# Six tiles of q and k in block 0: turned by VectorE in 32x32 blocks from finer loads, not by TensorE transposes with ScalarE copies

## The chip, the cores and the metric

One core of one Trainium2 chip. The metric is device time in microseconds (us). Engines are called TensorE (PE; its weight loads PEld), VectorE (DVE), ScalarE (ACT), GpSimd (POOL) and SyncE (SP, which here only issues DMAs).

## The reference, cut to what matters

```python
def sm_attn(qq, kk, vv):
    s = scale * np.matmul(qq, kk.transpose(0, 1, 3, 2))
    s = s - np.max(s, axis=-1, keepdims=True)
    a = np.exp(s)
    a = a / (np.sum(a, axis=-1, keepdims=True) + 1e-09)
    return np.matmul(a, vv)
p_packed = sm_attn(p, k, v)              # p: 8 x 8 heads x 32 x 64
out = sm_attn(q, p_packed, p_packed)     # q, k, v: 8 x 8 heads x 576 x 64
...
h = x @ w_in;  g = h / (1 + exp(-h));             x = g @ w_out      # first MLP
h = x @ w_in2; g = h * clip(h + 3, 0, 6) / 6;     y = g @ w_out2     # second MLP
```

x has 4608 rows of 512 numbers (8 batches x 576 positions, 8 heads x 64), and both MLPs widen it to 2048. All is float32.

## The kernel before, in words

The first MLP runs in nine blocks of 512 rows: block j takes the first 512 positions of batch j, the ninth the 64 left over from each batch. Within a block the 2048 wide columns go by in 16 steps f. hidden(f) makes 128 of them (lines 992 to 994, three products each, since every operand is kept as a high and a low part), ScalarE takes Silu (line 1001) and the high part gh (line 1008), VectorE the low part gl (line 1009), and two steps later projects(f) multiplies back into four accumulators (lines 1016 to 1018). Block 0 also makes the weights into high and low parts as it goes: for each f, ScalarE scales the raw words (lines 180 and 186), VectorE shifts and signs them (lines 195 and 199), GpSimd adds them (line 208), ScalarE rounds the sum to the high part (line 219) and VectorE subtracts (line 224). SyncE then stores the parts to memory for later blocks (line 215, tiles win, wo and wr). Each link waits for the one before it.

The attention of later batches is threaded through the blocks. A group n is four heads of a batch, so batch b has groups 2b and 2b+1. Groups 0 and 1 are done ahead of block 0; in block 0 comes the attention of groups 2 and 3, one after the other. A group has two tiles of q and two of k, each 128x512 for two heads. The steps of a group n in order: k is transposed and multiplied with p (scores), exponentials, the transposed weights a1 (tile T, made by line 431 through the copy of line 108), the products with v (lines 482 and 485), the packed keys, then q is transposed and multiplied with these, a second softmax, and the products that become x.

The class Plan places these steps between the MLP's products. A step has a place (a share of the block's products that must have gone by), needs (steps that must be so many products back), a tile limit and a number of PSUM banks that the planner's ring must have free. Four banks of tag h are shared by the hidden products and by all attention steps; a hidden bank comes free when gl of its step has been taken. What a step issues goes into its engines' in-order queues at that spot.

step_tr turns one tile of two heads (line 451). For groups up to 3 it takes four TensorE transposes into a PSUM bank (line 449) and a ScalarE copy to SBUF (line 108). For groups from 4 on it is one VectorE instruction that transposes each 32x32 block (line 456), which is the full transpose only because load_nat has put the 32x32 blocks where they belong: four DMAs of 32 partitions and 128-byte pieces (line 382) where the other form has two DMAs of 128 partitions and 256-byte pieces (line 386). The finer DMAs don't go out where load_nat is called: they stand in the list due, of which each tick of the planner issues one on SyncE's queue, and use() issues all that is left as long as the block is 0 or 1. SyncE also issues the weight stores and the loads of v. ScalarE issues the loads of raw weights in block 0 from its own queue (line 155).

Of the kernel before, what the change touches and what calls it, by code (L numbers as in the profile page):

```python
# [18 lines left out]
def tile_pack_attention_two_mlps(ctx: ExitStack, tc, q, k, v, p, w_in1, w_out1, w_in2, w_out2, out):  # L19
# [76 lines left out]
    def bank():  # L96

        pool, tag = (ps_h, "h")
        if early[0]:
            pool, tag = banks[0]  # L100
            banks.append(banks.pop(0))
        return pool.tile([P, T], F32, tag=tag, name="abank")
# [4 lines left out]
    def copy(out, in_):  # L107
        (nc.vector.tensor_copy if other[0] else nc.scalar.copy)(out=out, in_=in_)
# [10 lines left out]
    def half_kb(n, tag, bufs=1, what=""):  # L119

        if n == 1 or (n == 0 and what == "q"):
            pool, tag, n = spare.pop()
            if pool is xp:
                return pool.tile([P, T], F32, tag=tag, name="spare")
            if tag not in shared:
                shared[tag] = pool.tile([P, 2, T], F32, tag=f"wr{tag}", name="spare")
            return shared[tag][:, n]
        return at.tile([P, T], F32, tag=tag, name=tag, bufs=bufs)
# [222 lines left out]
    def ask(key=None):  # L351
        while due if key is None else any(k == key for k, _ in due):
            due.pop(0)[1]()
            if key is None:
                return
# [11 lines left out]
    def load_nat(n, what, j):  # L367
        src = {"k": k, "q": q, "v": v}[what]
        b, h0 = n // QPB, (n % QPB) * HQ + 2 * j
        m = half_kb(n, "nat", 2 * AHEAD, what)  # L370
        rows = src[b, h0:h0 + 2, 0:T, :]
        if what == "v":
            m = m.rearrange("p (h i d) -> p h i d", h=2, i=NI)
            load_queue[0].dma_start(out=m.rearrange("p h i d -> p h (i d)"), in_=rows.rearrange("h (p i) d -> p h (i d)", i=NI))
        elif n >= 4:

            g = m.rearrange("p (i b d) -> p i b d", i=NI, b=NI)
            for h in range(2):
                for e in range(2):
                    o = (2 * h + e) * NP  # L380
                    src = rows[h].rearrange("(b r i) d -> r i b d", b=NI, i=NI)[:, :, :, e * NP:(e + 1) * NP]
                    due.append(((what, n, j), lambda to=g[o:o + NP], src=src: nc.sync.dma_start(out=to, in_=src)))
        else:
            m = m.rearrange("p (i h d) -> p i h d", h=2, i=NI)
            for h in range(2):
                load_queue[0].dma_start(out=m[:, :, h, :], in_=rows[h].rearrange("(p i) d -> p i d", i=NI))
            m = m.rearrange("p i h d -> p i (h d)")
        nat[what, n, j] = m
# [58 lines left out]
    def turn_rows(ps, m):  # L447
        for i in range(NI):
            nc.tensor.transpose(ps[:, i * P:(i + 1) * P], m[:, i, :], ident)

    def step_tr(n, what, j):
        m = nat.pop((what, n, j))
        if n >= 4:
            ask((what, n, j))
            t = half_kb(n, "T", 5)
            nc.vector.transpose(out=t, in_=m)
            st[what, n, j] = t
            return
        ps = bank()
        turn_rows(ps, m)  # L460
        t = half_kb(n, "T", 5)
        copy(out=t, in_=ps)
        st[what, n, j] = t
# [117 lines left out]
    def step_u(n):  # L581
        ps = bank()
        nc.vector.transpose(out=ps, in_=d2s[n][:, 0:T])
        ah = at.tile([P, T], F32R, tag="a2h", name="a2h", bufs=3)
        al = at.tile([P, T], F32R, tag="a2l", name="a2l", bufs=3)
        copy(out=ah, in_=ps)
        nc.vector.tensor_sub(out=al, in0=ps, in1=f32(ah))
        st["a2", n] = ah, al

    def step_ut(n):  # L590
        assert st.pop("tails", None) is None
        st["tails"] = n
        for j in range(2):
            rows = slice(j * 64, (j + 1) * 64)
            nc.vector.transpose(out=tails[rows, j * TAIL:(j + 1) * TAIL], in_=d2s[n][rows, T:S])
# [128 lines left out]
    for j in range(2, B - 1):  # L724
        c, d = QPB * (j + 2), QPB * (j + 1)
# [14 lines left out]
    def load_next():  # L740

        while loaded[0] < len(uses) and (loaded[0] < AHEAD or uses[loaded[0] - AHEAD] in used):
            what, n = uses[loaded[0]]
            if what == "v" and any(w == "v" and (w, m) not in used for w, m in uses[:loaded[0]]):
                return
            loaded[0] += 1
            if what == "v" or what == "q" and n == QPB:
                load_tail(n, what)
            for j in range(2):
                load_nat(n, what, j)  # L750

    def use(what, n):
        used.add((what, n))
        load_next()
        while due and plan.block < 2:
            ask()
# [87 lines left out]
    def window(c, d, b, a, j, x):  # L844
# [6 lines left out]
        def add(n, what, cost, fn, *need, tile=None, bank=5, also=(), count=1):  # L851
            if n is not None:
                steps.append(((what, n), cost, fn, need, tile, bank, [k for k in also if k[1] is not None], count))
# [30 lines left out]
        add(c, "spread", 0, lambda: spread_p(c), ("kpq", b), bank=0)  # L884

        def turn():
            add(d, "q0", 0, lambda: step_tr(d, "q", 0), (("t", b if j == 1 else None), 0), bank=5 if j == 0 and (d or 9) < 4 else 0, tile=("z", d))
            add(d, "q1", 0, lambda: [step_tr(d, "q", 1), use("q", d)], ("q0", d), bank=5 if j == 0 and (d or 9) < 4 else 0, tile=("z", d))
            add(a, "u", 0, lambda: [step_u(a), step_ut(a)], before[1], (("t", b), 22 if j else 0), bank=15)
            add(c, "k0", 0, lambda: step_tr(c, "k", 0), (("q1", d), 0), (("t", b if j == 1 and d is not None else None), 20), bank=5 if j == 0 and (c or 9) < 4 else 0, tile=("s", c))  # L890
            add(c, "k1", 0, lambda: [step_tr(c, "k", 1), use("k", c)], ("k0", c), bank=5 if j == 0 and (c or 9) < 4 else 0, tile=("s", c))

        if j == 0:
            if b is not None:
# [2 lines left out]
            else:  # L897
                add(either, "kpq", 2, kpq, ("spread", c), bank=7)
            add(b, "pp", 4, lambda: step_pp(b), ("t", b), ("tt", b))
            turn()  # L900
            add(c, "s", 6, lambda: step_zs(c, None, None, None), ("k1", c), ("kpq", c), ("tt", b), bank=9, count=2, also=[("st", c)])
            add(b, "pt", 1, lambda: [alone(b, step_pt, step_ptc), use("v", b)], ("pp", b))
# [3 lines left out]
        else:  # L906
# [12 lines left out]
            if keys:  # L919
                n_banks = (b is not None) + (p0 is not None) + 1  # L920
                add(keys[0][1], keys[0][0], 2 * n_banks, transposes, before[0] if b is not None else ("spread", c), ("spread", c), ("pp", p0), tile=b is not None and ("pp", b),
                    bank=8, count=n_banks, also=keys[1:])
                add(x, "flush", 0, flush, ("xt", x), bank=0)
            b0 = b if j > 1 else None
            if j == 1:
                add(b, "pp", 4, lambda: step_pp(b), ("t", b), ("tt", b))
                p1 = b
            turn()

            def scores():  # L930
# [5 lines left out]
            if keys:  # L936
# [3 lines left out]
                    bank=9, also=keys[1:], count=n_banks)  # L940
# [765 lines left out]
    unit = [key for key in feed.keys]  # L1706

    load_nat(0, "k", 0)
    beside(load_p, 0)
    beside(load_nat, 0, "k", 1)  # L1710
    load_tail(0, "k")
    beside(load_nat, 1, "k", 0)
# [163 lines left out]
    for j in range(NBLK):  # L1876
        ws = WINDOWS[j] if j < len(WINDOWS) else []
        order = []
        n = QPB * (j + 1) - 1
# [118 lines left out]
```

## Time and profile before

| | |
|---|---|
| median of 3 runs | 1508.78 us (1508.05 to 1509.45) |
| the profiled execution: its own time, its span | 1509.61 us, 1507.8 us |
| busy in the span: PE, DVE, ACT, POOL | 98%, 69%, 52%, 13% |
| mean granted TensorE clock | 0.995 of full |

The span runs from the first to the last instruction; 1.8 us of the profiled execution's time lie around it. A matmul's row in the trace lasts longer than the distance to the next one, since matmuls are pipelined: how fast they go is read from their starts. Block 0 takes the stretch from about 36 to 160 us.

### The profile page before, as it was taken

The page shows a single profiled execution, that of the slowest core. Times are in us where ns is not written, and L with a number is a line of the kernel's source. Part 1 is how long each engine was busy: PE and PEld are TensorE (multiplying, and loading weights), DVE is VectorE, ACT ScalarE, POOL GpSimd, SP SyncE. Part 2 cuts the span into 40 slices and gives each one's busy share as a digit, 9 for nine tenths or more (in the row PEclk, how much of TensorE's full clock was granted, in tenths as well). Part 3 has the DMA queues.
Part 4 walks back from the last instruction along what each step waited for, and adds up shares of the span by engine and source line. Part 5 has one row for each costly group of instructions (what it writes and reads, how often), then busy time and mean ns, then how long its engine had stood idle before and what let it go on. Part 6 is the DMA issues. An engine that isn't in the chain of part 4 may idle for free.

```text
span 1507.8 us, 21726 instructions
## 1 busy us (share of the span) xinstructions
PE 1483.1 (98%) x7550; PEld 1230.3 (82%) x7550; DVE 1036.0 (69%) x1695; ACT 779.4 (52%) x1241; POOL 192.5 (13%) x177
## 2 busy tenths in 40 slices
PE   7999999999999999999999999999999999999998
PEld 4777777777777778788878888888888888999998
DVE  6767466756575656653463779786978687778767
ACT  6876657655566456655452344334433443444443
POOL 2433011111211211123240000000000000000000
PEclk9999999999999999999999999999999999999999
DMA  9999789997698769868895576678667866997987
GB/s 246 306 306 276 247 214 253 274 253 198 177 245 263 199 165 306 231 178 239 243 291 178 193 225 216 195 216 252 219 193 223 242 215 210 286 313 255 271 273 226
DMA packets 434509, 358.52 MB, mean 238 GB/s; under 512 B 191200, under 2 KB 325856, under 8 KB 434400
## 3 DMA queue, kind: packets, MB, share of 16 engines
q1 hardware_dynamic: 422832, 343.59, 77.6%
q10 hardware_dynamic: 11568, 13.54, 2.9%
q8 instruction: 61, 1.00, 0.3%
q14 instruction: 48, 0.39, 0.1%
HBM read 295.17 MB, written 61.87 MB: 237 GB/s over the span
## 4 chain that ended last, share of the span: by engine, by line
PE 84%; ACT 6%; DMA 4%; DVE 3%; SPq 2%; issue 1%; POOL 1%; ACTq 0%; POOLq 0%; DVEq 0%
PE b L1270 8%; PE b L1268 8%; PE b L1269 8%; PE b L1363 8%; PE b L1366 7%; PE b L1365 7%; PE acc L1016 7%; PE acc L1017 7%; PE acc L1018 7%; PE hps L992 4%; PE hps L993 4%; PE hps L994 4%; DMA wo<-w1o 1%; DMA praw<-in_moe_w_out_dram 1%; PE abank L524 1%
## 5 line engine op out<-in xcount | busy, mean ns | idle before, releaser
L1009 DVE TENSOR_TENSOR gl<-hps,gh 128x512 fp32r<-128x512 f32 x144 | 98.9, 687 | 190.6 <-ACT gh L1008 187.8
L1366 PE MATMUL b<-ro,ws 128*128 128x512 f32 (+2 forms) x564 | 206.4, 366 | 0.0
L1365 PE MATMUL b<-ro,ws 128*128 128x512 f32 (+2 forms) x564 | 206.3, 366 | 0.0
L1268 PE MATMUL b<-xc,ws 128*128 128x512 f32 (+1 forms) x560 | 205.7, 367 | 0.0
L1270 PE MATMUL b<-xc,ws 128*128 128x512 f32 (+1 forms) x560 | 205.7, 367 | 0.0
L1269 PE MATMUL b<-xc,ws 128*128 128x512 f32 (+1 forms) x560 | 205.7, 367 | 0.0
L1311 DVE TENSOR_TENSOR ro<-g,ro 128x1024 fp32r<-128x1024 f32 (+1 forms) x140 | 161.5, 1158 | 41.5 <-ACT ro L1306 41.2
L1306 ACT CAST ro<-g 128x1024 fp32r<-128x1024 f32 (+1 forms) x140 | 132.0, 967 | 93.4 <-DVE g L1299 34.5
L1001 ACT ACTIVATE hps<-hps 128x512 f32<-128x512 f32 x144 | 83.9, 583 | 116.0 <-PE hps L994 115.0
L1363 PE MATMUL b<-ro,ws 128*128 128x512 f32 (+2 forms) x564 | 138.9, 367 | 0.3
L1366 PEld LDWEIGHTS b<-ro,ws 128*128 128x128 f32 x564 | 105.9, 188 | 13.1
L1365 PEld LDWEIGHTS b<-ro,ws 128*128 128x128 f32 x564 | 105.9, 188 | 13.1
L1268 PEld LDWEIGHTS b<-xc,ws 128*128 128x128 f32 x560 | 105.1, 188 | 13.2
L1269 PEld LDWEIGHTS b<-xc,ws 128*128 128x128 f32 x560 | 105.1, 188 | 13.2
L1016 PE MATMUL acc<-gh,wo 128*128 128x512 f32 x288 | 114.6, 398 | 1.3 <-DMA wo<-w1o 1.3
L1270 PEld LDWEIGHTS b<-xc,ws 128*128 128x128 f32 x560 | 105.1, 188 | 13.0
L1363 PEld LDWEIGHTS b<-ro,ws 128*128 128x128 f32 x564 | 102.9, 188 | 15.0 <-DVE ro L1311 2.1
L1016 PE MATMUL acc<-gh,wr 128*128 128x512 f32 x288 | 114.0, 396 | 0.5 <-ACT gh L1008 0.5
L1017 PE MATMUL acc<-gl,wr 128*128 128x512 f32 x288 | 112.5, 391 | 0.2 <-DVE gl L1009 0.2
L1018 PE MATMUL acc<-gh,wr 128*128 128x512 f32 x288 | 112.5, 390 | 0.0
L1018 PE MATMUL acc<-gh,wo 128*128 128x512 f32 x288 | 112.4, 390 | 0.0
L1017 PE MATMUL acc<-gl,wo 128*128 128x512 f32 x288 | 112.4, 390 | 0.0
(310 smaller groups left out, 2899.4 us busy)
## 6 DMA issues: line engine op xcount, KB each, us to landing
ws<-w2in SPq DMA_DIRECT2D x280, 256.0 KB, 3.3
ws<-w2out SPq DMA_DIRECT2D x280, 256.0 KB, 3.5
wi<-w1i SPq DMA_DIRECT2D x80, 512.0 KB, 6.6
wo<-w1o SPq DMA_DIRECT2D x64, 512.0 KB, 6.2
x1d<-x SPq DMA_DIRECT2D x18, 512.0 KB, 5.2
w1i<-win SPq DMA_DIRECT2D x16, 512.0 KB, 7.2
praw<-in_moe_w_in_dram SPq DMA_DIRECT2D x32, 256.0 KB, 6.2
praw<-in_moe_w_out_dram SPq DMA_DIRECT2D x32, 256.0 KB, 5.7
```

The source lines that it names most:

```text
L1009: nc.vector.tensor_sub(out=gl, in0=g, in1=f32(gh))
L1016: mm(acc[e], lhsT=w[:, 0, s], rhs=gh, start=first, stop=False)
L1017: mm(acc[e], lhsT=w[:, 0, s], rhs=gl, start=False, stop=False)
L1018: mm(acc[e], lhsT=w[:, 1, s], rhs=gh, start=False, stop=last)
L1268: mm(ps, lhsT=wh, rhs=xs[k][:, 0, c], start=first, stop=False, skip_group_check=True)
L1269: mm(ps, lhsT=wh, rhs=xs[k][:, 1, c], start=False, stop=False, skip_group_check=True)
L1270: mm(ps, lhsT=wl, rhs=xs[k][:, 0, c], start=False, stop=last, skip_group_check=True)
L1306: nc.scalar.copy(out=t[:, 0], in_=v)
L1311: nc.vector.tensor_sub(out=t[:, 1], in0=self.operand(s), in1=f32(t[:, 0]))
L1363: mm(to, lhsT=wh, rhs=x, start=False, stop=last, skip_group_check=True)
L1365: mm(to, lhsT=wh, rhs=x, start=first, stop=False, skip_group_check=True)
L1366: mm(to, lhsT=wl, rhs=x, start=False, stop=False, skip_group_check=True)
```

## The change

The tiles of q and k of group 3 and of q of group 2 (two tiles each, six in all) take the form that groups from 4 on have: finer loads through the list due, one VectorE transpose each, no TensorE transposes, no ScalarE copy. Their steps no longer ask the planner for a bank. k of group 2 stays as it was. The loads of q of group 2, which were issued ahead of block 0, now go out one at a time in the first ticks of block 0.

```diff
@@ load_nat
-        elif n >= 4:
+        elif n >= 3 or (what, n) == ("q", 2):
 
             g = m.rearrange("p (i b d) -> p i b d", i=NI, b=NI)
             for h in range(2):
@@ step_tr
         m = nat.pop((what, n, j))
-        if n >= 4:
+        if n >= 3 or (what, n) == ("q", 2):
             ask((what, n, j))
             t = half_kb(n, "T", 5)
             nc.vector.transpose(out=t, in_=m)
@@ window, turn
-            add(d, "q0", 0, lambda: step_tr(d, "q", 0), (...), bank=5 if j == 0 and (d or 9) < 4 else 0, tile=("z", d))
-            add(d, "q1", 0, lambda: [step_tr(d, "q", 1), use("q", d)], ("q0", d), bank=5 if j == 0 and (d or 9) < 4 else 0, tile=("z", d))
+            add(d, "q0", 0, lambda: step_tr(d, "q", 0), (...), bank=0, tile=("z", d))
+            add(d, "q1", 0, lambda: [step_tr(d, "q", 1), use("q", d)], ("q0", d), bank=0, tile=("z", d))
...
-            add(c, "k0", 0, lambda: step_tr(c, "k", 0), (...), bank=5 if j == 0 and (c or 9) < 4 else 0, tile=("s", c))
-            add(c, "k1", 0, lambda: [step_tr(c, "k", 1), use("k", c)], ("k0", c), bank=5 if j == 0 and (c or 9) < 4 else 0, tile=("s", c))
+            add(c, "k0", 0, lambda: step_tr(c, "k", 0), (...), bank=5 if j == 0 and c == 2 else 0, tile=("s", c))
+            add(c, "k1", 0, lambda: [step_tr(c, "k", 1), use("k", c)], ("k0", c), bank=5 if j == 0 and c == 2 else 0, tile=("s", c))
```

## Rows read from the trace of the kernel before

**Rows 1.** Busy time by engine, TensorE's granted clock, DMA share, GB/s, two stretches.
```profile
36.00:160.00 124.00, 118.67 (x609) 91.81 (x608) 89.62 (x159) 93.78 (x171) 45.98 (x39) 0.96 0.97 293
160.00:700.00 540.00, 535.03 (x2896) 419.65 (x2895) 334.26 (x691) 322.77 (x547) 96.78 (x96) 1.00 0.83 229
```

**Rows 2.** Waits of TensorE, 38 to 160 us: total, times, longest.
```profile
PE abank L449 <- DVE gl L1009: 4.6, 2, 2.3
```

**Rows 3.** Timeline of TensorE, 71 to 80 us: start, length, idle before and its releaser.
```profile
71.61 0.39 PE L994 MATMUL hps<-xh,win 128*128 128x512 f32 x1
74.32 0.66 PE L449 MATMUL abank<-ident,nat 128*128 128x128 f32 x4 [2.32 <-DVE gl L1009]
...
76.88 1.08 PE L482 MATMUL abank<-nat,T 128*32 128x64 f32 x32
...
78.26 1.41 PE L449 MATMUL abank<-ident,nat 128*128 128x128 f32 x8
79.42 0.48 PE L992 MATMUL hps<-xh,win 128*128 128x512 f32 x1
```

**Rows 4.** Timeline of TensorE around one group of four transposes.
```profile
81.11 0.39 PE L1017 MATMUL acc<-gl,wr 128*128 128x512 f32 x1
81.33 0.40 PE L1018 MATMUL acc<-gh,wr 128*128 128x512 f32 x1
81.57 0.60 PE L449 MATMUL abank<-ident,nat 128*128 128x128 f32 x4
...
82.24 0.39 PE L1017 MATMUL acc<-gl,wr 128*128 128x512 f32 x1
```

**Rows 5.** Timeline of TensorE, 112 to 121 us.
```profile
112.00 0.60 PE L413 MATMUL abank<-ident,d 128*128 128x128 f32 x4
...
118.51 0.66 PE L449 MATMUL abank<-ident,nat 128*128 128x128 f32 x4 [2.27 <-DVE gl L1009]
...
120.93 1.08 PE L482 MATMUL abank<-nat,T 128*32 128x64 f32 x32
```

**Rows 6.** Timeline of ScalarE, 74 to 119 us.
```profile
74.17 0.58 ACT L108 COPY T<-abank 128x512 f32<-128x512 f32 x1
...
103.95 0.62 ACT L219 CAST win<-cr 128x512 fp32r<-128x512 f32 x1 [2.78 <-POOL cr L208]
...
114.64 0.58 ACT L108 COPY T<-abank 128x512 f32<-128x512 f32 x1
...
118.17 0.58 ACT L108 COPY T<-abank 128x512 f32<-128x512 f32 x1
```

**Rows 7.** VectorE's block transposes in later blocks, ns min/median/max (line 456).
```profile
L456 DVE STREAM_TRANSPOSE T<-nat x48: 660/693/711, 157.2 to 621.5; 128x512 f32<-128x512 f32 x48
```

**Rows 8.** Timeline of VectorE at the two spots where transposes come.
```profile
76.98 0.69 DVE L224 TENSOR_TENSOR wo<-cr,wo 128x512 fp32r<-128x512 f32 x1 [1.32 <-ACT wo L219]
...
117.77 0.69 DVE L1009 TENSOR_TENSOR gl<-hps,gh 128x512 fp32r<-128x512 f32 x1 [1.56 <-ACT gh L1008]
```

**Rows 9.** Timeline of SyncE's DMA issues: start, time taken, count.
```profile
41.40 5.89 SPq L386 DMA_DIRECT2D nat<-in_k_dram  x4
...
80.22 2.62 SPq L386 DMA_DIRECT2D nat<-in_q_dram  x4
82.94 8.99 SPq L382 DMA_DIRECT2D nat<-in_k_dram  x8
...
94.50 1.78 SPq L215 DMA_DIRECT2D w1i<-win  x2
```

**Rows 10.** The chain that ended last, its piece at 47 us.
```profile
47.39 7.36 DMA w1i<-win
```

**Rows 11.** Waits of ScalarE, 24 to 130 us: total, times, longest.
```profile
ACT wo L219 <- DMA nat<-in_k_dram: 1.4, 1, 1.4
```

**Rows 12.** DMA issues, 24 to 130 us: count, KB each, median us to landing.
```profile
nat<-in_q_dram SPq DMA_DIRECT2D x8, 128.0 KB, 4.3
...
nat<-in_k_dram SPq DMA_DIRECT2D x8, 64.0 KB, 6.8
```

More of the change, by code (lines that the diff above doesn't have):

```diff
@@ L886, in turn @@
         def turn():
-            add(d, "q0", 0, lambda: step_tr(d, "q", 0), (("t", b if j == 1 else None), 0), bank=5 if j == 0 and (d or 9) < 4 else 0, tile=("z", d))
-            add(d, "q1", 0, lambda: [step_tr(d, "q", 1), use("q", d)], ("q0", d), bank=5 if j == 0 and (d or 9) < 4 else 0, tile=("z", d))
+            add(d, "q0", 0, lambda: step_tr(d, "q", 0), (("t", b if j == 1 else None), 0), bank=0, tile=("z", d))
+            add(d, "q1", 0, lambda: [step_tr(d, "q", 1), use("q", d)], ("q0", d), bank=0, tile=("z", d))
             add(a, "u", 0, lambda: [step_u(a), step_ut(a)], before[1], (("t", b), 22 if j else 0), bank=15)
-            add(c, "k0", 0, lambda: step_tr(c, "k", 0), (("q1", d), 0), (("t", b if j == 1 and d is not None else None), 20), bank=5 if j == 0 and (c or 9) < 4 else 0, tile=("s", c))
-            add(c, "k1", 0, lambda: [step_tr(c, "k", 1), use("k", c)], ("k0", c), bank=5 if j == 0 and (c or 9) < 4 else 0, tile=("s", c))
+            add(c, "k0", 0, lambda: step_tr(c, "k", 0), (("q1", d), 0), (("t", b if j == 1 and d is not None else None), 20), bank=5 if j == 0 and c == 2 else 0, tile=("s", c))
+            add(c, "k1", 0, lambda: [step_tr(c, "k", 1), use("k", c)], ("k0", c), bank=5 if j == 0 and c == 2 else 0, tile=("s", c))
         if j == 0:
```

## Prediction

> **What bounds the kernel.** I read the table of stretches first [rows 1]. After 160 us TensorE is busy 535 of 540 us at full clock: what is gained earlier is carried to the end, unless something else catches it. In 36 to 160 us, block 0, where all six tiles are turned, TensorE is busy 118.7 of 124 us at a mean granted clock of 0.96 (of 2.4 GHz), and ScalarE and VectorE are busy for about three quarters. So I read what TensorE waited for there [rows 2]: 4.6 us in two waits, both of the transposes of line 449, both for gl. A transpose reads no gl. What it waits for is its PSUM bank, which the hidden product of the step before still holds until VectorE has read it. The two spots are in [rows 3] and [rows 5]. At the first, TensorE starts its last product at 71.61 and the transposes of q of group 2 at 74.32. At the second, transposes of q of group 3 start at 118.51 after 2.27 us. Both times gl is late because ScalarE has changed over to the exponential and back. Its timeline shows the second case best [rows 6]: before the cast at 103.95 it waited 2.78 us for GpSimd, and in the 24 rows from there to the copy at 118.17 none has idle time before it. There ScalarE sets the pace, not TensorE.
>
> Both spots are followed by the products with v (line 482), which read the copy a1 that ScalarE makes at 74.17 and at 118.17 [rows 6].
>
> **TensorE's own work.** A product starts 0.22 to 0.23 us after the one before. From 81.33 to 82.24 there are two such steps and one group of four transposes [rows 4]: 0.91 - 2 x 0.23 = 0.45 us for a group. Four groups are like it, or stand at the waits. The eight transposes at 78.26 hold the next product until 79.42, so 1.16 us [rows 3], more than twice 0.45; the wait is just behind them, and I read it as part of the clock that the stretch's mean of 0.96 has lost [rows 1]. Sum: 4 x 0.45 + 1.16 = 3.0 us less for TensorE. That is the gain if TensorE alone set the pace, with the waits as they are.
>
> **The two waits.** They don't go away, they move. A step of a transpose counts nothing in the planner, so the products with v stay at the same tick, nine products into the hidden step: three before the first wait, six after. Without transposes TensorE runs these six in the time in which it stood, until about 71.84 + 6 x 0.23 = 73.2, and then waits for a1, copied by 74.17 + 0.58 = 74.75. The products with v began at 76.88, so they come 2.1 us earlier. Then 1.16 and 0.45 us of transposes are gone, and TensorE leads by 3.7 us at 83. At the second spot the products with v can't begin before a1 is copied, 118.17 + 0.58 = 118.75, where they began at 120.93: 2.2 us. The lead of 3.7 us is not added. TensorE comes early to the transposes that it did at 112.00 and to a1, and waits for ScalarE there. What counts at the end is the second spot alone: 2.2 us, plus what ScalarE's own chain has gained or lost by then.
>
> **ScalarE's chain.** Six copies go, 0.58 us each. The one at 114.64 lies ahead of a1 in the stretch without idle time, so a1 comes 0.6 us earlier. The copy after a1 is hidden. The four around 77 to 82 lie ahead of the 2.78 us wait for GpSimd at 103.95, so they count only through the weight chain (scaled by ScalarE, shifted by VectorE, added by GpSimd, cast by ScalarE). There they are 2.3 us less. But VectorE now has four transposes at one tick, since no bank spaces them: 4 x 0.69 = 2.8 us [rows 7], in the queue ahead of the wo subtraction at 76.98, where VectorE idled for 1.32 us [rows 8]. They delay it and the shifts behind it by 2.8 - 1.32 = 1.4 us or so; behind the shifts wait GpSimd, ScalarE's next cast and the next gl. I take 0 for the two together, with ends of -1.4 and +2.3 us. The two transposes of q of group 3 come before the gl that waited 1.56 us at 117.77 [rows 8]: 1.4 us, hidden. If that cover were gone they would cost 1.4.
>
> The Trainium skill, in "VectorE: DVE Perf Modes", "Rules for kernel authors", says to use TensorE for a 128x128 transpose if PSUM will do as the destination. The rows give TensorE 0.45 us against VectorE's 0.69 for a tile, so counted as equal engine time the exchange would lose 6 x 0.24 = 1.4 us. That count leaves out the bank and the copy, which I expect to matter more.
>
> **The loads.** Six tiles had two DMAs each and now have four: 24 for 12, in 128-byte pieces. SyncE issued eight such pieces of k for group 4 in 8.99 us where four of the old form took 2.62 us, when no buffer held them [rows 9]. The pieces landed after 6.8 us with half the bytes, against 4.3 us [rows 12]. While they were under way ScalarE's own load of weights stood 1.4 us for one of them [rows 11], and the weight stores came only at 94.50 [rows 9]. For q of group 2 I take nothing: the eight go out in the first ticks of block 0, ahead of the loads of k of group 3, which wait for buffers until 41.40 [rows 9], and are needed at about 71. For k of group 3, four took 5.89 us; eight may take 8.99, so the store of win behind them, at 47.39 in the chain that ended last [rows 10], comes up to 3.1 us later, and ScalarE's next cast with it. For q of group 3, between 2.62 us twice and 8.99 us: 2.6 to 6.4 us more on SyncE's queue, ahead of the loads of k of group 4 and the weight stores. But that queue starts 2.1 us sooner, since the loads of v ahead of it wait for the products with v. A store issued at 94.50 lands after some 7.36 us, by 101.9; the cast at 103.95 that writes to one of the three buffers has 2.1 us to spare. Bounds: nothing, or 3.1 + (6.4 - 2.1) = 7.4 us on ScalarE's chain. The waits that the chain has at 91.9 and 103.95 swallow the first of it, so I take 0.6 us, near the lower end. That is a choice, and the weakest one here.
>
> **Sum.** 2.2 (second spot) + 0.6 (copy ahead of it) + 0 (VectorE against copies) - 0.6 (loads) = 2.2 us. The profiled execution took 1509.61 us, so 1507.4; the median of the runs is 0.8 us lower, so 1506.5 us, 0.15% faster. A measurement of this kernel tells about 0.2%, 3 us, from no change: this is inside it.
>
> **Rivals.**
> *ScalarE's chain gains as well.* If the four copies count in full, and the transposes and loads are hidden, a1 comes 2.3 us sooner again, 2.2 + 0.6 + 2.3 = 5.1: 1503.7 us. For it: ScalarE has no idle time in the stretch that decides. Against: the 2.78 us wait for GpSimd ahead of it. In the extreme both waits vanish with the clock's fall after them and the transposes: 3.0 + 4.6 + the lost clock, 0.04 x 124 = 5 us, makes 12.6 us. The reading of a1 excludes it.
> *The loads hold the weight chain: slower.* SyncE's queue is held by q of group 3 so that the store of win comes more than 2.1 us after 94.50, ScalarE's cast waits for the buffer, and all behind it moves. With 3.1 us at 47 us and 4.3 at 94.50, less the 2.1 to spare, 5.3 us are lost against 2.8 won: +2.5, 1511.3 us. It decides against the change once the chain is more than 2.8 us late at the second spot. For it: the wait in [rows 11] and the landing times. Against: no DMA wait of TensorE in block 0 [rows 2]. The Trainium skill, in "DMA: Bandwidth & Descriptors", "Specifications", asks for transfers of at least 512 bytes for line rate. By it 128 bytes are worse than 256, and the landing times agree.
> *Hidden anyway.* The wait reappears in full at the products with v, or a later one takes back what is left: 1508.8 us, within 0.5.
>
> **How the numbers follow.** The forecast, 1505.8 to 1508.3 on its own: 0.40. ScalarE's gain: 0.36. Hidden: 0.12. Loads: 0.12. The range reaches to 1503 for the first rival's 5.1 us and a little over, and to 1510.3 on the other side; a bit under 2 in 10 stays outside, most of it the loads at full price. Faster by over 0.2%: 0.38, the first rival and the lower edge of the forecast. Slower: 0.10, most of the loads. The rest, 0.52, is within 0.2%.
>
> **What would show it.** No wait of line 449 for gl in block 0, but waits of line 482 for ScalarE's a1: about 1.5 us at the first spot, more at the second and at the transposes of line 413 ahead of it. Products with v near 74.8 and 118.7 us. Six new transposes of some 0.69 us on VectorE, four in a row. SyncE: eight issues for k of group 3 by 50 us, the store of win behind them not over 3 us later; weight stores of 94.50 within 2 us. The prediction is wrong if the second a1 copy moves by more than 1 us either way, if the transposes wait for loads, or if the planner, with more banks free, puts other steps elsewhere.

## The result and the profile after

The change makes the kernel slower: a median of 1516.62 us (1515.48 to 1520.04, 6 runs) against 1508.5 us of the kernel before (6 runs), a ratio of 1.0055 [1.0044, 1.0065] (in brackets, here and below, the 95% interval), so 8.1 us. The forecast was 1506.5 us. The profiled execution of the changed kernel took 1518.54 us, with a span of 1516.7 us.

The table of stretches of the kernel after answers to [rows 1] (columns: busy time of PE, PEld, DVE, ACT and POOL with their instructions, granted clock, DMA share, GB/s):

```profile
36.00:160.00 124.00, 110.56 (x546) 84.41 (x545) 87.25 (x155) 83.42 (x154) 45.52 (x38) 0.93 0.99 280
160.00:700.00 540.00, 534.77 (x2894) 418.75 (x2893) 335.74 (x693) 325.49 (x550) 95.21 (x95) 1.00 0.83 228
```

The second stretch is as it was. In the first, block 0, TensorE is busy 8.1 us less than before, and the block ends 8.6 us later: the first Silu (line 1001) of block 1 starts at 163.93 us, where it started at 155.31. Where in the block the time goes is seen by following that one instruction, step f by step f. These are its starts in four traces (`e1_coarse` and `e2_fine` are told below), with the distance to before:

| Silu of step | before | after | e1_coarse | e2_fine |
|---|---|---|---|---|
| 2 | 52.54 | 52.09 (-0.5) | 51.72 (-0.8) | 53.23 (+0.7) |
| 3 | 58.69 | 63.44 (+4.8) | 59.11 (+0.4) | 64.41 (+5.7) |
| 6 | 80.40 | 82.77 (+2.4) | 78.44 (-2.0) | 85.24 (+4.8) |
| 9 | 99.97 | 102.92 (+3.0) | 98.17 (-1.8) | 105.37 (+5.4) |
| 10 | 107.24 | 116.07 (+8.8) | 105.56 (-1.7) | 117.05 (+9.8) |
| 11 | 116.53 | 124.78 (+8.3) | 116.75 (+0.2) | 126.28 (+9.8) |
| 12 | 126.25 | 135.59 (+9.3) | 127.56 (+1.3) | 136.13 (+9.9) |
| first of block 1 | 155.31 | 163.93 (+8.6) | 155.85 (+0.5) | 165.17 (+9.9) |

Two jumps, ahead of steps 3 and 10, and between them 2.4 us won back. So I read what TensorE and ScalarE waited for in block 0. TensorE's waits of the kernel after, from 30 to 170 us (us in total, times, longest):

```profile
PE hps L992 <- ACT win L219: 6.1, 2, 3.5
PE abank L1678 <- ACT a2h L1665: 3.3, 2, 2.0
PE abank L482 <- ACT T L108: 2.8, 1, 2.8
PE hps L992 <- DVE gl L1009: 1.8, 2, 1.1
```

The two waits of line 449 for gl [rows 2] are gone, and a wait of line 482 for ScalarE's a1 has come, as forecast. Above them stands something new: the hidden product waits 6.1 us for win, which ScalarE casts. ScalarE's own waits, from 24 to 170 us, say why:

```profile
ACT win L219 <- POOL cr L208: 9.9, 7, 2.3
ACT win L219 <- DMA w1i<-win: 8.6, 1, 8.6
ACT a2h L108 <- DVE abank L583: 7.1, 2, 4.2
ACT win L219 <- DMA pn<-in_p_dram: 6.3, 1, 6.3
```

The cast waits 8.6 us once for a store of win, and 6.3 us once for what the profile calls a load of p. Their places in ScalarE's timeline:

```profile
59.59 0.62 ACT L219 CAST win<-cr 128x512 fp32r<-128x512 f32 x1 [6.28 <-DMA pn<-in_p_dram]
...
112.73 0.62 ACT L219 CAST win<-cr 128x512 fp32r<-128x512 f32 x1 [8.61 <-DMA w1i<-win]
```

These are the two jumps. A cast doesn't read pn: that load was issued at 57.38 and landed 2.23 us later, at 59.61, just as the cast began, and the profile names what landed last. What the cast needs is one of win's three buffers, and a buffer is held until its store has landed. SyncE's timeline shows when the stores were issued:

```profile
33.67 4.20 SPq L382 DMA_DIRECT2D nat<-in_q_dram  x5
38.77 0.64 SPq L215 DMA_DIRECT2D w1i<-win  x1
45.96 1.96 SPq L382 DMA_DIRECT2D nat<-in_q_dram  x3
48.02 7.56 SPq L382 DMA_DIRECT2D nat<-in_k_dram  x8
55.68 0.63 SPq L215 DMA_DIRECT2D w1i<-win  x1
57.38 0.33 SPq L393 DMA_DIRECT2D pn<-in_p_dram  x1
...
83.86 10.15 SPq L382 DMA_DIRECT2D nat<-in_q_dram  x8
94.11 9.48 SPq L382 DMA_DIRECT2D nat<-in_k_dram  x8
104.10 0.37 SPq L215 DMA_DIRECT2D w1o<-wo  x1
104.79 2.34 SPq L215 DMA_DIRECT2D w1i<-win  x2
```

The store of win that was issued at 47.39 [rows 10] now comes at 55.68, behind q of group 2 and k of group 3. Between 39.41 and 45.96 SyncE stands at the sixth piece of q of group 2; the profile puts 6.5 us of this to the landing of a load of raw weights. The store of 94.50 [rows 9] comes at 104.79, behind q of group 3, which goes out 3.6 us later than before (83.86 against 80.22) and takes 10.15 us where its four coarse loads took 2.62. The chain of work that ended last has this store and the cast in it:

```profile
104.79 7.87 DMA w1i<-win
112.73 0.63 ACT win L219
```

The rest of the changed parts, VectorE's transposes by line and in its timeline:

```profile
L456 DVE STREAM_TRANSPOSE T<-nat x54: 660/696/712, 80.4 to 630.7; 128x512 f32<-128x512 f32 x54
```
```profile
80.36 0.71 DVE L456 STREAM_TRANSPOSE T<-nat 128x512 f32<-128x512 f32 x1
...
84.25 1.30 DVE L456 STREAM_TRANSPOSE T<-nat 128x512 f32<-128x512 f32 x2
...
86.81 0.70 DVE L456 STREAM_TRANSPOSE T<-nat 128x512 f32<-128x512 f32 x1
```

Six more than before, of the duration forecast, but one, two and one around 80 to 87 us, not four in a row.

### The profile page after: what moved, and what is told of

Same layout as the page of the kernel before. It is cut to its first block, busy times and chain, and to the rows that moved or that the text cites. A ratio compares the mean times of both kernels' runs of the same rounds, so it can differ in the third digit from the quotient of the medians.

```text
span 1516.7 us, 21692 instructions
## 1 busy us (share of the span) xinstructions
PE 1481.7 (98%) x7526; PEld 1228.4 (81%) x7526; DVE 1037.4 (68%) x1701; ACT 776.0 (51%) x1235; POOL 193.3 (13%) x177
## 4 chain that ended last, share of the span: by engine, by line
PE 83%; DMA 5%; ACT 4%; DVE 3%; SPq 2%; issue 1%; POOL 0%; ACTq 0%; DVEq 0%; POOLq 0%
PE b L1270 8%; PE b L1269 8%; PE b L1268 8%; PE b L1363 8%; PE b L1366 7%; PE b L1365 7%; PE acc L1016 7%; PE acc L1017 7%; PE acc L1018 7%; PE hps L992 4%; PE hps L994 4%; PE hps L993 4%; DMA wi<-w1i 1%; DMA raw<-in_moe_w_in_dram 1%; PE abank L682 1%
```

## The experiments

Two theories stood against each other. *The queue*: the twelve additional DMAs stand ahead of the stores of win in SyncE's in-order queue; ScalarE's cast is late, and with it TensorE; the exchange of engines costs nothing. *The exchange*: VectorE's transposes in the weight chain, and TensorE's lost work, cost the time, and the stores are late because the steps are. Kernels e1 to e4 ran on one chip, e5 to e8 on another, e9 to e12 on a third, each time beside the kernel before (medians 1508.98, 1508.32 and 1509.2 us). Ratios are to it. Some kernels turn tiles that have not been laid out for it; they do the same amount of work on elements in another order.

**The exchange alone** (against the kernel after; loads as before, in their old places):

```diff
-        elif n >= 3 or (what, n) == ("q", 2):      # load_nat
+        elif n >= 4:
-            nc.vector.transpose(out=t, in_=m)
+            nc.vector.transpose(out=t, in_=m if n >= 4 else m.rearrange("p i e -> p (i e)"))
```

> The VectorE transposes, without copies and banks, on tiles that come by the two coarse loads of before, in their old places (the elements of q and k are then in other places than the reference has them). If the loads alone cost the 8 us (the stores of win stand behind them on SyncE's queue, and ScalarE waits for a buffer of win), this is faster than before by the 2 to 5 us that the exchange was forecast to gain: 1503.5 to 1506.5, with no wait of ScalarE for a store over 2 us in block 0. If the four VectorE transposes in a row, or steps that the planner moved for want of banks, hold the weight chain, it stays near 1514 to 1516.6.

1510.52 us, 1.0005 [0.9995, 1.0015]. The stores of win are at 47.46 and 93.69 again, and the loss is gone. But there is no gain either. TensorE's timeline shows the products with v where the prediction put them:

```profile
75.25 0.65 PE L482 MATMUL abank<-nat,T 128*32 128x64 f32 x32 [1.42 <-ACT T L108]
...
119.22 1.08 PE L482 MATMUL abank<-nat,T 128*32 128x64 f32 x32 [4.83 <-ACT T L108]
```

The lead of 1.7 to 2.0 us that the table shows from step 6 to step 10 is lost at 11 and 12. ScalarE's timeline there:

```profile
102.27 0.62 ACT L219 CAST win<-cr 128x512 fp32r<-128x512 f32 x1 [2.88 <-DMA w1i<-win]
...
111.09 0.62 ACT L219 CAST win<-cr 128x512 fp32r<-128x512 f32 x1 [1.57 <-POOL cr L208]
...
113.69 0.62 ACT L219 CAST wr<-cr 128x512 fp32r<-128x512 f32 x1 [0.86 <-DMA w1i<-win]
...
118.59 0.58 ACT L108 COPY T<-abank 128x512 f32<-128x512 f32 x1
...
127.07 0.59 ACT L108 CAST a2h<-abank 128x512 fp32r<-128x512 f32 x1 [4.59 <-DVE abank L583]
```

In the stretch in which ScalarE had no idle time [rows 6] it now waits for GpSimd's sum and for a store, and comes to the copy of a1 0.4 us later than before. The two waits, 1.57 + 0.86 us, less the copy of 0.58 us that is gone, are the 1.9 us that step 11 loses. Then it waits 4.59 us for VectorE, which works without a gap from 117.98 to 127.04, one of the transposes among its work:

```profile
121.95 0.70 DVE L456 STREAM_TRANSPOSE T<-nat 128x512 f32<-128x512 f32 x1
...
126.33 0.71 DVE L583 STREAM_TRANSPOSE abank<-d 128x512 f32<-128x512 f32 x1
```

**The loads alone** (against the kernel before; TensorE transposes, copies and banks as they were):

```diff
-        elif n >= 4:                               # load_nat
+        elif n >= 3 or (what, n) == ("q", 2):
...
+        if n >= 3 or (what, n) == ("q", 2):        # step_tr, ahead of the TensorE transposes
+            ask((what, n, j))
+            m = m.rearrange("p (i e) -> p i e", i=NI)
```

> The finer loads alone, with the TensorE transposes, copies and banks of before (elements in other places than the reference has them). If the loads cost it all, this is as slow as the changed kernel or slower, 1516 to 1520, with the two long waits of ScalarE's cast near 59 and 112 us. If the transposes on VectorE do, it is within 2 us of before, 1507 to 1510.

1517.91 us, 1.0055 [1.0038, 1.0071]: the whole loss, without any of the exchange. ScalarE's waits are those of the kernel after:

```profile
ACT win L219 <- DMA w1i<-win: 7.2, 1, 7.2
ACT win L219 <- DMA pn<-in_p_dram: 6.1, 1, 6.1
```

**The same DMAs, issued one a tick.** In the kernel after, use() empties the list due at once in block 0; here only in block 1, so that other issues come between:

```diff
-        while due and plan.block < 2:
+        while due and plan.block == 1:
```

> The changed kernel, but in block 0 the list of finer loads is no longer emptied at once: one DMA goes out at each tick, so that the stores of win come in between. If the order on SyncE's queue is what costs, the stores are issued within 3 us of before's 47.4 and 94.5, and the time falls to 1506 to 1511. If the DMA engines' work on twice as many pieces costs, it stays at 1514 to 1518.

1512.34 us, 1.002 [1.0009, 1.0031]: over half of the loss goes, with as many DMAs of the same form. SyncE's timeline has stores among the pieces:

```profile
48.08 0.58 SPq L382 DMA_DIRECT2D nat<-in_k_dram  x1
48.76 0.63 SPq L215 DMA_DIRECT2D w1i<-win  x1
49.45 4.96 SPq L382 DMA_DIRECT2D nat<-in_k_dram  x3
...
92.63 1.08 SPq L215 DMA_DIRECT2D w1i<-win  x1
```

The stores of 47.4 and 94.5 are back within 3 us, but the time is 1.3 us above the range that was expected for it. In what is left, 0.2%, the trace has smaller waits of ScalarE's casts: 1.98 us for a store at 56.13, 2.25 us for GpSimd at 63.45, 1.85 us for a store at 74.60. Which of them counts was not tested.

**Which tiles.** Three kernels keep the form after for some tiles only: without q of group 2, with k of group 3 alone, with q of group 3 alone (conditions in load_nat and step_tr, banks as before for the others):

```diff
-        elif n >= 3 or (what, n) == ("q", 2):
+        elif n >= 3:                               # e4_no_q2
+        elif n >= 4 or (what, n) == ("k", 3):      # e5_k3_only
+        elif n >= 4 or (what, n) == ("q", 3):      # e6_q3_only
```

> The changed kernel with q of group 2 as before: coarse loads ahead of block 0, TensorE transposes, copies and banks. In the changed kernel the sixth of its eight pieces stood 6.5 us on SyncE's queue for a landing, ahead of the loads of k of group 3. If that moved load costs, the store of win at 55.7 comes 4 to 7 us sooner and the time falls by 2 to 5 us, to 1512 to 1515. If only the number of pieces of k and q of group 3 matters, or ScalarE's second wait alone sets the end, it stays within 1.5 us of 1516.6.

1516.71 us, 1.0052 [1.0037, 1.0067]. q of group 2 adds nothing that can be measured to the other two, though its pieces stood 6.5 us on the queue: without them k of group 3 takes 11.90 us from 41.31, and the store still comes only at 53.31. That is 2.4 us sooner than in the kernel after, but ScalarE's cast starts at 59.59 in both: what the cast needs is the store's landing, and that came no sooner.

> Only k of group 3 is changed (finer loads, VectorE, no bank); both tiles of q stay as before. If its eight pieces ahead of the store of win near 47 us cost, the store comes 4 to 6 us later than 47.4 and ScalarE waits over 3 us near 55; if that delay is lost for good, 1511 to 1514. If it is caught up at later waits, as the run without q of group 2 suggests that one early delay was, 1508 to 1510.

1513.3 us, 1.004 [1.0027, 1.0054]; stores at 52.02 and 98.42; step 3 is 3.7 us late.

> Only q of group 3 is changed. Its eight pieces go out together with the eight of k of group 4, ahead of the stores that before were issued at 94.5. If that queue sets the loss, the stores come after 100 us, ScalarE waits over 4 us for one near 105 to 112, and the time is 1512 to 1516. If the early loads of k of group 3 set it, this is within 2 us of before.

1514.18 us, 1.0034 [1.0019, 1.005]; stores at 48.11 and 102.40; step 9 is 0.1 us late, step 10 5.5. Each of the two makes its own jump, at its own store. Together they cost 0.55%, by the middle values less than 0.40 + 0.34; the intervals leave a plain sum open.

**How many, or how small.** Two kernels from e1_coarse part the two properties of the finer form. One has four DMAs for a tile, in the large pieces of 256 bytes, through due; the other two DMAs for a tile, in pieces of 128 bytes, at the old place:

```diff
+                for e in range(2):                 # e7_four_wide, in load_nat
+                    o, src = slice(64 * e, 64 * e + 64), rows[h].rearrange("(p i) d -> p i d", i=NI)
+                    if n >= 3 or (what, n) == ("q", 2):
+                        due.append(((what, n, j), lambda to=m[o, :, h, :], src=src[o]: nc.sync.dma_start(out=to, in_=src)))
...
+                if n >= 3 or (what, n) == ("q", 2):    # e8_two_small, in load_nat
+                    to = m.rearrange("p i h d -> p (i h d)").rearrange("p (g h d) -> p g h d", g=2 * NI, h=2)
+                    src = rows[h].rearrange("(p i) (e d) -> p (i e) d", i=NI, e=2)
+                    load_queue[0].dma_start(out=to[:, :, h, :], in_=src)
+                    continue
```

> As the run with coarse loads and VectorE transposes, but each tile comes in four DMAs of 64 partitions with pieces of 256 bytes, by the list and in the order of the changed kernel (elements in other places than the reference has them). If the number of DMAs on SyncE's queue and in flight is what costs, this is as slow as the changed kernel, 1514 to 1518. If the 128-byte pieces cost, it is as fast as the coarse loads, 1508 to 1511.

1514.49 us, 1.0047 [1.0033, 1.0062]. SyncE's timeline:

```profile
48.62 6.84 SPq L389 DMA_DIRECT2D nat<-in_k_dram  x8
55.55 0.63 SPq L215 DMA_DIRECT2D w1i<-win  x1
...
85.56 7.91 SPq L389 DMA_DIRECT2D nat<-in_q_dram  x8
93.57 8.13 SPq L382 DMA_DIRECT2D nat<-in_k_dram  x8
...
103.23 2.06 SPq L215 DMA_DIRECT2D w1i<-win  x2
```

At the first spot, where the profile of the kernel after names the load of p, ScalarE's timeline here names the store:

```profile
61.17 0.62 ACT L219 CAST win<-cr 128x512 fp32r<-128x512 f32 x1 [6.70 <-DMA w1i<-win]
```

> As the run with coarse loads and VectorE transposes, with two DMAs for each tile in the old places, but pieces of 128 bytes (elements in other places than the reference has them). If the number of DMAs costs, this stays at 1508 to 1511. If the small pieces cost, 1514 to 1518, and the loads of q and k land after 6 us or more instead of about 4 to 5.

1509.59 us, 1.0008 [0.9998, 1.0018]. SyncE's timeline:

```profile
39.58 6.53 SPq L389 DMA_DIRECT2D nat<-in_k_dram  x4
46.20 0.92 SPq L215 DMA_DIRECT2D w1i<-win  x1
...
92.98 2.58 SPq L215 DMA_DIRECT2D w1i<-win  x2
```

So small pieces cost nothing that can be measured, beside e1_coarse's 1.0005; four DMAs in place of two, through due, cost 0.4%. The traces confirm that the two properties were parted: from 24 to 130 us they count 22994 packets under 512 bytes in e8_two_small, near the 23139 of the kernel after, and 17008 in e7_four_wide, near the 16877 of e1_coarse. What no run parts is the number from the way through due, since e7_four_wide has both; a kernel with two DMAs for a tile through due is missing.

**Is the order of due worth something by itself?** The edit of e3_trickle in the kernel before, and in e1_coarse:

> The kernel before, but in block 0 the finer loads that it has (k of group 4 and those that follow) go out one at a tick. Before, eight of them held SyncE's queue from 82.9 to 91.9, ahead of the stores at 94.5. If the stores held back there cost the kernel before as well, it gets 1 to 4 us faster, 1504.5 to 1507.5. If the stores had slack there (2 us were reckoned), it stays within 1 us of 1508.5.

1509.62 us, 0.9995 [0.9983, 1.0007]: nothing, where no additional pieces stand ahead of the stores. So what e3_trickle won is put down to the stores, not to another order of the rest.

> The run with coarse loads and VectorE transposes, with the same one at a tick for k of group 4 (elements in other places than the reference has them). The lead of 1.8 us that TensorE had in steps 6 to 9 was lost by step 12; ScalarE waited 2.9 us for a store of win on the way. If that wait took it back, this is 2 to 4 us faster than the coarse run, 1504.5 to 1507. If VectorE's stretch without idle time after 118 us took it, it stays at 1508 to 1510.5.

1508.98 us, 0.9992 [0.9982, 1.0002]. The wait of 2.88 us for a store ahead of step 10 is gone; ahead of step 11 ScalarE still waits 1.89 us for GpSimd and 0.89 us for a store. Step 11 is 0.9 us late, and step 12 1.95 us, with ScalarE waiting 4.58 us for VectorE. Its time can't be told from before or, by its interval, from e1_coarse: inconclusive.

**Another queue.** The finer pieces of groups 2 and 3 issued by GpSimd in block 0:

```diff
-    due.append((..., lambda to=g[o:o + NP], src=src: nc.sync.dma_start(out=to, in_=src)))
+    due.append((..., lambda to=g[o:o + NP], src=src: (nc.gpsimd if plan.block == 0 and n < 4 else nc.sync).dma_start(out=to, in_=src)))
```

> The changed kernel, its finer loads of groups 2 and 3 issued on GpSimd's queue in place of SyncE's. If SyncE's queue alone is what costs, the stores of win keep before's times within 2 us and the time falls to 1506 to 1511. If the GpSimd instructions behind the issues (the additions of the weight chain) are held instead, or the number of DMAs in flight counts whichever queue they are on, it stays at 1514 or more.

1567.5 us, 1.039 [1.0376, 1.0404]: the second case, and far beyond it. GpSimd's timeline and ScalarE's waits:

```profile
75.47 0.71 POOL L382 DMA_DIRECT2D nat<-in_k_dram  x1 [1.94 <-issue]
78.24 0.71 POOL L382 DMA_DIRECT2D nat<-in_k_dram  x1 [2.06 <-issue]
```
```profile
ACT win L219 <- POOL cr L208: 73.2, 9, 29.0
```

An issue every 2.7 us on the engine that adds the weights; 24 of them hold it some 65 us, and the time rises by 58. So this run says nothing on whether SyncE's queue alone is what costs.

**The exchange without q of group 3** (from e1_coarse; these two tiles on TensorE, with bank and copy):

```diff
-        if n >= 3 or (what, n) == ("q", 2):        # step_tr
+        if n >= 4 or (what, n) in (("q", 2), ("k", 3)):
```

> The run with coarse loads, but q of group 3 is turned by TensorE with its bank and copy as before; q of group 2 and k of group 3 stay on VectorE (elements of these in other places than the reference has them). If VectorE's stretch after 118 us takes the lead back because two more transposes stand in it, the second wait is again for gl and this is 0.5 to 1.5 us faster than the coarse run. If the lead was lost before that, it is the same within 0.5 us.

1511.02 us, 1.0008 [0.9999, 1.0016]. ScalarE's wait ahead of step 12 is that of before again:

```profile
125.24 0.59 ACT L108 CAST a2h<-abank 128x512 fp32r<-128x512 f32 x1 [3.24 <-DVE abank L583]
```

The lead is 2.8 us at step 10, 0.5 at 11, 0.5 at 12, and 0.15 at the first Silu of block 1. So in the trace the transposes of q of group 3 cost 1.1 to 1.3 us at step 12; the larger loss, at step 11, is there without them. In the time this shows nothing.

## Why the prediction was wrong

**The loads: the step that failed.** "The waits that the chain has at 91.9 and 103.95 swallow the first of it, so I take 0.6 us, near the lower end." Measured alone, in e2_fine, the loads cost 0.55%, 8.3 us (5.7 to 10.7 by the interval): about the upper bound of 7.4, not 0.6. The prediction called this its weakest choice, and both parts of it were too low. It let the first store come up to 3.1 us later, from eight issues at the pace of [rows 9]; it came 8.3 us later, with q of group 2 taken back 5.9. It let the second come up to 4.3 us later, since that queue would start 2.1 us sooner; it came 10.3 us later. After the first jump the loads of q of group 3 started 3.6 us later, not sooner, and took 7.5 us more. With q of group 3 alone, in e6_q3_only, they took 6.4 us more, the most that was reckoned, but started 1.3 us later, and the store came 7.9 us later. Then it let waits swallow the delay, but ScalarE's cast is stopped until the store has landed, 6.3 and 8.6 us long. The clue was in the rows shown: the store of 47.39 with its 7.36 us stands in the chain that ended last [rows 10], so no delay of it was free. ScalarE's timeline before has the cast that already waited for it:

```profile
54.82 0.62 ACT L219 CAST win<-cr 128x512 fp32r<-128x512 f32 x1 [1.09 <-DMA w1i<-win]
```

e3_trickle, e5_k3_only and e6_q3_only show that most of the cost is the place ahead of the stores, and e7_four_wide and e8_two_small that it is the larger number of DMAs, issued at once through due, and not the size of their pieces. The Trainium skill, in "DMA: Bandwidth & Descriptors", "Specifications", asks for 512 bytes for line rate; here halving 256 to 128 bytes made no difference that can be measured.

**The slower rival** had the mechanism as it is: the store late, the cast waiting for the buffer, all behind it moved. It was priced at 1511.3 us and given 0.12. Its price used the same 3.1 and 4.3 us, and took off 2.8 us of gains that did not come. What was put against it, no DMA wait of TensorE in block 0 [rows 2], was no evidence: TensorE waits for ScalarE, and ScalarE for the DMA.

**q of group 2, taken as nothing:** by e4_no_q2 it is nothing in the time, though not for the reason given. Its pieces did not all go out in the first ticks; three went out only from 45.96 on, ahead of k of group 3.

**The two waits move, they don't go away:** right. By e1_coarse the products with v start at 75.25 after 1.42 us (forecast 74.8 after about 1.5) and at 119.22 (118.75). TensorE's lead of 3.7 us forecast for 83 us was too large: Silu of step 6 is 2.0 us earlier.

**The gain of 2.2 + 0.6 us at the second spot:** wrong, and the loads are not the reason. The products with v do start 1.7 us sooner in e1_coarse. But what follows does not depend on them: ScalarE and its weight chain set the pace of steps 11 and 12. "What counts at the end is the second spot alone" is the sentence that failed. ScalarE reached a1 0.4 us later than before, not 0.6 sooner, since it waited for GpSimd and for a store in a stretch that had been without idle time; and q of group 3's transposes, "hidden", fell partly behind the gl of 117.98, where VectorE has no idle time: the price of 1.4 us without cover is near the 1.1 to 1.3 found. Which of GpSimd and the store holds step 11 first was not told apart; e10_coarse_trickle, without the store's wait ahead of step 10, has both waits ahead of step 11 and is late at 11 and 12 as well.

**VectorE's four transposes against the four copies, taken as 0:** they did not come in one row, and no run measured the two alone. With the loads of before the whole exchange changes the time by +0.05% [-0.05, 0.15], which is no change that can be told. That is the third rival, "hidden anyway", for this part. The Trainium skill, in "VectorE: DVE Perf Modes", "Rules for kernel authors", prefers TensorE for a transpose of 128x128; counted as engine time that was 1.4 us of loss, which this interval neither shows nor excludes.

## What to carry to other kernels

Ahead of a change that adds DMAs, read what stands behind them on the issuing engine's queue. A store that frees a buffer is latency-critical even if nobody reads what it stores: if it is in the chain that ended last, issues put ahead of it can cost their time in full, as far as they make it land later. Split such a group with the store in between, or, where the layout allows, keep the number of DMAs and change the form of each.

When a wait of the busiest engine is removed, ask which engine is without idle time in the same stretch: the lead lasts only until that one is needed.

## What the hardware showed beyond that

In the kernel after, eight DMAs in a row on SyncE's queue took 7.56 to 10.15 us, 0.95 to 1.27 us for each, where one alone took 0.6 us. In the row of 10.15 us the median issue took 0.71 us and the longest 1.89; the rest are waits between them.

Issued by GpSimd, the 64 KB loads of k landed after a median of 2.4 us and those of q after 2.9, against 5.9 and 5.8 from SyncE in the kernel after, but each took GpSimd 2.7 us. The queue is not shown to be the reason: the DMA engines were 57% busy there in 36 to 160 us, against 99%, and from 24 to 300 us of the same run 64 KB loads issued by SyncE landed after 2.6 and 2.8 us.

TensorE's granted clock in 36 to 160 us did not follow its idle time alone: 0.96 before with 5.3 us idle, 0.93 in the kernel after with 13.4 us, and 0.99 in e1_coarse with 11.0 us, where the time was nevertheless that of before.
